# A changed start-up order in a tuned FFT-and-MLP kernel: table first, expanded matrices on two engines, weight clamp and second weight fold later

## Chip, cores and metric

One core of one Trainium2 chip. The metric is the device time of the core in microseconds (us); lower is better. The kernel before took 1937.98 us (median of 3 runs, 1937.06 to 1938.95). Ratios are the mean time of one kernel's fast runs over the mean of the other's fast runs of the same rounds, so they are not quite the ratio of the medians that are quoted; the interval in brackets is the 95% interval. Absolute times of different batches come from different chips, so every batch has its own runs of the kernel before.

## The reference

```python
x:     (8, 3008, 256)   float32
w_in:  (256, 2048),  w_out: (2048, 256)

X = np.fft.fft(x, axis=1)
X = np.fft.fft(X, axis=2)
y = X.real.astype(np.float32).reshape(8 * 3008, 256)

h = y @ w_in
g = h * (1.0 / (1.0 + np.exp(-1.702 * h)))
return (g @ w_out).astype(np.float32)          # (24064, 256)
```

The kernel does the long transform in two stages (3008 = 47 x 64), folds the short transform into `w_in` ahead of time ("weight folds"), and runs 384 hidden/activation/product steps. Nearly the whole run is those steps on TensorE. This study is about the first 80 us, in which the first transform stage, the rounding of the weights and the weight folds are done.

## The kernel before

These are the parts that the change and the argument touch. `pair` holds the expanded matrices of the first mixing, `room` the folded pieces of x.

```python
def matrices():                                     # 8 expanded matrices from the first table
    kinds = [w0[:, n0 + i:n0 + i + 1] for i in range(3)]
    tasks = iter((nc.scalar, nc.gpsimd, nc.vector) * 4)
    for s0, own, other in ((1, 0, 1), (17, 1, 0)):
        src = w0[:, s0 * NM:(s0 + 15) * NM].rearrange("p (s m) -> p s m", m=NM)
        for even in (1, 0):
            for c, kind in enumerate((own, other)):
                ...                                 # one scaled copy, 128 x 720, on next(tasks)

def fold_first(g):
    t, e = xt[0:2 * NA, 4 * g:4 * g + 4, :], room[g][0:2 * NA]
    nc.gpsimd.tensor_copy(free(e, 0, [D, 4], [H, 2]), free(t, 0, [D, 4], [H, 2]))   # corner copy, 94 x 8
    for at, op in ((1, ALU.add), (H + 1, ALU.subtract)):
        nc.vector.tensor_tensor(e[:, :, at:at + H - 1], t[:, :, 1:H],
                                free(t, D - 1, [D, 4], [-1, H - 1]), op=op)

def mix_first(i):                                   # 8 matmuls, then one copy by ScalarE
    ps, ns = bank("ps1"), (2 * i + 1, 2 * i + 2) if i < 7 else (0, 15)
    ...
    nc.scalar.copy(to, free(ps[:], 0, [D, 2], [1, D]))

def bounds(key, first=False):                       # "the clamp" of one weight chunk
    ...
    nc.gpsimd.tensor_scalar(m[:], hi, scalar1=TOP, scalar2=-TOP, op0=ALU.min, op1=ALU.max)   # m
    if first:
        nc.vector.tensor_tensor(g[:], hi, hi, op=ALU.mult)                                   # g
    else:
        nc.scalar.activation(g[:], hi, ACTF.Square)                                          # g
    nc.scalar.activation(r[:].bitcast(F32), lo, ACTF.Copy, scale=2.0 ** -29, bias=2.0 ** 23) # r
    nc.scalar.activation(r[:], r[:].bitcast(F32), ACTF.Copy, bias=-2.0 ** 23)                # r

# rounded(): m, a, a on VectorE; finish(): wst = a + r on GpSimd

def fold_w(n):                                      # psw: 4 matmuls; wcs copies; psf: 4; af copy
    for cs in range(2):
        ps = bank("psw")
        for i in range(2):
            nc.tensor.matmul(ps[:], lhsT=cd[:, i, cs, :], rhs=wst[n][:, i, :], start=(i == 0), stop=(i == 1))
        nc.scalar.copy(wcs[cs][...], ...)
    ps = bank("psf")
    for f in range(4 * n, 4 * n + 4):               # weights with a single row
        nc.tensor.matmul(ps[:, f:f + 1], lhsT=wcs[1][0:1, f * 128:f * 128 + 128], rhs=twos[:], ...)
    nc.scalar.copy(af2[:, 4 * n:4 * n + 4], ps[:, 4 * n:4 * n + 4])

def nyquist(b, blk):                                # for the first block only:
    row = pqt[b, blk][0:1, 1, :]
    ps = bank("psn")
    nc.tensor.matmul(ps[:], lhsT=ones[:], rhs=row, start=True, stop=True)    # ones is 1 x 128
    nc.scalar.copy(nb[:], ps[:])
```

The start-up order:

```python
nc.scalar.dma_start(out=w0, in_=tab1[:, 0:n0 + 4])            # first table, 802 KB
for part in ((0, 4), (28, 32), (4, 8), (24, 28), (8, 16), (16, 24)):
    load_first(*part)                                         # x, on SyncE's queue
...
warm(7)
matrices()
for i, need in enumerate(((0, 7), (1,), (6,), (2,), (5,), (3,), (4,), ())):
    for g in need:
        fold_first(g)
    mix_first(i)
    ...
    if i == 4:
        bounds(("in", 0), True)                               # clamp of chunk 0 inside the mixing
...                                                           # spills, refill
round_in(0)
finish_in(0)
bounds(("in", 1), True)
round_in(1)
finish_in(1)
fold_w(0)
warm(3)
bounds(("out", 0))
round_out(0)
finish_out(0)
rotate(0, 0, 4)                                               # the small copy t
stage2(0, 0)                                                  # transform of the first block: pq
fold_w(1)
bounds(("in", 2))
...
ahead = [("in", 2), ("out", 1), ("in", 3), ("out", 2), ("out", 3)]
for t, (kind, c) in enumerate(ahead):
    at(t, round_out if kind == "out" else round_in, c)
    if t + 1 < len(ahead):
        at(t, bounds, ahead[t + 1])
    at(t + 1, finish_out if kind == "out" else finish_in, c)
early[2], early[4] = 2, 3                                     # folds 2 and 3 inside the step loop
```

In the step loop, step t does: hidden(t) (pa, pb on TensorE, v on ScalarE); nyquist if t is 0; product; `fold_w(early[t])`; activate; rows(t) (h, dif, h on VectorE, which free the banks pa and pb); then what `at` put there.

Of the kernel before, what the change touches and what calls it, by code (L numbers as in the profile page):

```python
# [35 lines left out]
NJ = NB // 2  # L36
NM = 48
# [9 lines left out]
def view(ap, offset, *dims):  # L47
    return bass.AP(ap.tensor, ap.offset + offset, [list(d) for d in dims])


def free(ap, offset, *dims):
    return bass.AP(ap.tensor, ap.offset + offset, [list(ap.ap[0])] + [list(d) for d in dims])
# [8 lines left out]
def tables(S, D):  # L61

    assert S == NA * NB and D == 256
    H = D // 2
    ks = np.array([kp(u, a) for a in range(NG) for u in range(NU)])
    s = NB * np.arange(NA)[:, None, None] + np.arange(NB)[None, :, None]
    angle = 2.0 * np.pi * ((s * ks) % S) / S
    cos, sin = np.cos(angle), np.sin(angle)
    w1 = np.zeros((NA, NJ + 3, NG * NU, 2))
    w1[:, 1:NJ, :, 0], w1[:, 1:NJ, :, 1] = cos[:, 1:NJ], sin[:, 1:NJ]  # L70
    e0, o0, e1, o1 = ENDS
    w1[:, e0, :, 0], w1[:, o0, :, 0], w1[:, e1, :, 1], w1[:, o1, :, 1] = cos[:, 0], sin[:, 0], cos[:, NJ], sin[:, NJ]


    w0 = np.zeros((128, NJ + 1, NG * NU, 2))
    low, high = w0[0:2 * NA:2], w0[1:2 * NA:2]
    low[:] = w1[:, :NJ + 1]
    high[:, 1:NJ, :, 0], high[:, 1:NJ, :, 1] = cos[:, NJ + 1:], -sin[:, NJ + 1:]
    high[:, e0, :, 1], high[:, o0, :, 1] = cos[:, NJ], sin[:, NJ]
    odd = np.arange(128)[:, None] % 2  # L80
    kinds = np.concatenate([1.0 - odd, odd, -1.0 * odd, 1.0 - 2.0 * odd], 1)

    c, q = np.divmod(np.arange(NJ), 16)
    m2 = []
    for jj in np.where(q, np.where(c, NJ - q, q), 16 * c), 4 * (q // 2) + 2 * (q % 2) + c:
        j, k2 = jj[:, None], np.arange(NB)[None, :]
        beta = 2.0 * np.pi * ((j * k2) % NB) / NB
        m = np.zeros((NU, 2, NJ, 2, NB))
        m[:, 0, :, 0], m[:, 1, :, 0] = np.cos(beta), -np.sin(beta)
        m[:, 0, :, 1], m[:, 1, :, 1] = np.sin(beta), np.cos(beta)  # L90
        m[:, :, 0, 0] = m[:, :, 0, 1] = np.stack([np.ones(NB), 1.0 - 2.0 * (np.arange(NB) % 2)])
        m2.append(m)
    rot = np.zeros((NU, 2, NJ, NU, 2, NJ))
    for i in range(NU):
        for n in range(NJ):
            rot[i, 0, n, i, 1, n], rot[i, 1, n, i, 0, n] = (1.0, -1.0) if n else (0.0, 0.0)
        rot[i, 0, 0, i, 0, 0] = rot[i, 1, 0, i, 1, 0] = 1.0

    m, d = np.arange(D)[:, None], np.arange(H)[None, :]
    phi = 2.0 * np.pi * ((m * d) % D) / D  # L100
    cd = np.stack([np.cos(phi), -np.sin(phi)], 1)
    cd[:, 1, 0] = 1.0 - 2.0 * (np.arange(D) % 2)
    cd = cd.reshape(2, H, 2, H).transpose(1, 0, 2, 3)
    small = [t.reshape(128, -1) for t in (*m2, rot, cd)]
    pad = 64 - NM
    w1 = np.pad(w1.reshape(NA, -1), ((0, 128 - NA), (0, pad)))
    w0 = np.concatenate([w0.reshape(128, -1), np.zeros((128, pad)), kinds], 1)
    return np.concatenate([w0, w1], 1).astype(np.float32), np.concatenate(small, 1).astype(np.float32)
# [3 lines left out]
def kernel(ctx: ExitStack, tc, x, w_in, w_out, tab1, tab2, out):  # L112
    nc = tc.nc
    B, S, D = x.shape
# [19 lines left out]
    Td = [nc.dram_tensor(f"Td{b}", (NG * 128, D), F32, kind="Internal").ap() for b in range(B)]  # L134
# [18 lines left out]
    def bank(name):  # L153
        return psm.tile([128, 512], F32, tag="mm", name=name)
# [6 lines left out]
    xt = xp.tile([128, NJ, D], F32, tag="x", name="xt")  # L161
# [69 lines left out]
    def matrices():  # L231

        kinds = [w0[:, n0 + i:n0 + i + 1] for i in range(3)]
        tasks = iter((nc.scalar, nc.gpsimd, nc.vector) * 4)
        for s0, own, other in ((1, 0, 1), (17, 1, 0)):
            src = w0[:, s0 * NM:(s0 + 15) * NM].rearrange("p (s m) -> p s m", m=NM)
            for even in (1, 0):
                for c, kind in enumerate((own, other)):
                    out, by = pair[:, even, s0:s0 + 15, c * NM:(c + 1) * NM], kinds[kind if even or not kind else 2]
                    eng = next(tasks)  # L240
                    if eng is nc.scalar:
                        eng.activation(out, src, ACTF.Copy, scale=by)
                    else:
                        eng.tensor_scalar(out, src, scalar1=by, scalar2=None, op0=ALU.mult)  # L244
# [14 lines left out]

    def mix_first(i):  # L260

        ps, ns = bank("ps1"), (2 * i + 1, 2 * i + 2) if i < 7 else (0, 15)
        for at, n in enumerate(ns):
            for even in range(2):
                c0, c1 = (0, H + 1) if even else (H + 1, D)
                o = ps[:, at * D + c0:at * D + c1]
                for k, slot in enumerate((n, NJ - n if n else 16)):
                    rhs = room[slot // 4][:, slot % 4, c0:c1]
                    w = free(pair[:, even, slot], 0, [1, 128])
                    nc.tensor.matmul(o, lhsT=w, rhs=rhs, start=(k == 0), stop=(k == 1))  # L270
        to = free(xt[:], ns[0] * D, [(ns[1] - ns[0]) * D, 2], [1, D])
        nc.scalar.copy(to, free(ps[:], 0, [D, 2], [1, D]))

    def spill_first(lo, hi):
        for c, eng in enumerate((nc.sync, nc.scalar)):
            eng.dma_start(out=view(Td[0], (16 * c + lo) * D, [NJ * D, NM], [1, (hi - lo) * D]),
                          in_=xt[NM * c:NM * c + NM, lo:hi, :].rearrange("p q d -> p (q d)"))

    def load_matrices():
# [74 lines left out]
    def bounds(key, first=False):  # L354


        hi, lo = raw[key][:, :, 1].bitcast(F32), raw[key][:, :, 0]
        g = sp.tile([128, 1024], F32, tag="s", bufs=3, name="g")
        m = cv.tile([128, 1024], F32, tag="m", bufs=2, name="m")
        r = cv.tile([128, 1024], U32, tag="r", bufs=2, name="r")  # L360
        nc.gpsimd.tensor_scalar(m[:], hi, scalar1=TOP, scalar2=-TOP, op0=ALU.min, op1=ALU.max)  # L361

        if first:
            nc.vector.tensor_tensor(g[:], hi, hi, op=ALU.mult)
        else:
            nc.scalar.activation(g[:], hi, ACTF.Square)
        nc.scalar.activation(r[:].bitcast(F32), lo, ACTF.Copy, scale=2.0 ** -29, bias=2.0 ** 23)
        nc.scalar.activation(r[:], r[:].bitcast(F32), ACTF.Copy, bias=-2.0 ** 23)
        pre[key] = g, m, r
# [22 lines left out]
    def round_in(n):  # L392
        wst[n] = op.tile([128, 2, 512], F32, tag="os", name="wst")
        out = wst[n][:].rearrange("p i f -> p (i f)")
        last["in", n] = rounded(lambda *ins: [(out, ins)], ("in", n))
# [10 lines left out]
    def finish_in(n):  # L406
        last["in", n]()
# [177 lines left out]
    n0 = (NJ + 1) * NM + 64 - NM  # L585
    flat = wot[:].rearrange("p w a q n -> p (w a q n)")
    pair = flat[:, 0:2 * NJ * 2 * NM].rearrange("p (e s m) -> p e s m", e=2, s=NJ)
    w0 = flat[:, 6176:6176 + n0 + 4]
# [5 lines left out]
    nc.vector.memset(wcs[0][:, 0:512], 1.0)  # L594
    for i, e in enumerate(rooms):

        (nc.vector, nc.gpsimd)[i % 2].memset(e[64:128], 0.0)
    nc.vector.memset(flat[:, 6144:6176], 0.0)
    nc.vector.memset(free(pair[:, 0, 0], 0, [2 * NJ * NM, 2], [16 * 2 * NM, 2], [1, 2 * NM]), 0.0)
    nc.vector.memset(ones[:], 1.0)  # L600
    nc.vector.memset(twos[:], 2.0)
    nc.scalar.dma_start(out=w0, in_=tab1[:, 0:n0 + 4])
    for part in ((0, 4), (28, 32), (4, 8), (24, 28), (8, 16), (16, 24)):
        load_first(*part)
    load_in(0, nc.sync)
# [6 lines left out]
# [4 lines that stand above are left out]
        if i == 2:  # L616
            specials()
        if i == 3:
            spill_first(1, 9)
            load_out(0, nc.sync)  # L620
        if i == 4:
            bounds(("in", 0), True)
        if i == 5:
            spill_first(9, 13)
    spill_first(13, 16)
    spill_first(0, 1)
    fill(0, 0, 4)
    load_in(2, nc.sync)
    load_out(1, nc.sync)
    round_in(0)  # L630
    finish_in(0)
    bounds(("in", 1), True)
    round_in(1)
    finish_in(1)
    fold_w(0)
    warm(3)
    bounds(("out", 0))
# [1 line left out]
    finish_out(0)  # L639
    rotate(0, 0, 4)  # L640
    stage2(0, 0)
    fold_w(1)
    bounds(("in", 2))

    extra, early = {}, {}

    def at(t, fn, *args):
        extra.setdefault(t, []).append((fn, args))

    n = len(steps)  # L650

    ahead = [("in", 2), ("out", 1), ("in", 3), ("out", 2), ("out", 3)]
    for t, (kind, c) in enumerate(ahead):
        at(t, round_out if kind == "out" else round_in, c)
        if t + 1 < len(ahead):
            at(t, bounds, ahead[t + 1])
        at(t + 1, finish_out if kind == "out" else finish_in, c)
    early[2], early[4] = 2, 3
    at(1, fill, 0, 4, NG)
    for t, load, c in ((0, load_in, 3), (1, load_out, 2), (2, load_out, 3)):  # L660
        at(t, load, c, nc.sync)
# [76 lines left out]
```

## Time and profile before

| kernel before | value |
|---|---|
| median of 3 runs | 1937.98 us |
| span of the profiled execution | 1935.6 us |
| TensorE idle in it | 21.6 us |
| mixing ends / first r / first fold starts | 33.3 / 28.5 / 33.3 us |
| hidden group 0 / v of step 1 / third fold | 50.5 / 58.0 / 62.4 us |
| hidden group 3, from where TensorE hardly stops | 69.4 us |

How to read it: in the chain of waits each line is start, duration, engine, tile and line of the kernel; each piece was released by the one above it. The timeline's lines are start, busy time, engine, line, operation, tiles, shapes, and in brackets the idle time before it with what ended it. "DVE" is VectorE, "ACT" ScalarE, "POOL" GpSimd, "PE" TensorE; psw is a weight fold. Each matmul of the code stands as two records in these traces (`warm(7)` shows as x14), and counts such as x8 are of records. A granted clock of 1.00 is full, 0.50 is half. A bank is an output buffer of the matmuls; a spill writes mixed rows to DRAM, and the refill reads them back. The lines themselves are in the prediction below.

### The profile page before, as it was taken

What the parts mean: (1) busy time and instruction counts of PE and PEld (TensorE: products, weight loads), DVE (VectorE), ACT (ScalarE), POOL (GpSimd) and SP (SyncE); (2) the same over time, 40 slices, a digit from 0 to 9 for tenths busy, and PEclk for the clock granted to TensorE, in tenths of its full rate; (3) what the DMA queues carried; (4) which work ended last, traced back from release to release, by engine and by line L of the source; (5) the groups of instructions that cost most, each with busy time, mean ns of one, the idle gap of its engine ahead of it and who ended that gap; (6) DMA issues with size and microseconds to landing.
All of it is one profiled execution on the core that took longest, in us unless ns stands there. A gap on an engine that the chain in (4) does not pass through costs nothing.

```text
span 1935.6 us, 29331 instructions
## 1 busy us (share of the span) xinstructions
PE 1914.0 (99%) x10722; PEld 1680.3 (87%) x10722; DVE 1417.6 (73%) x2935; ACT 670.4 (35%) x920; POOL 771.3 (40%) x1064
## 2 busy tenths in 40 slices
PE   8899999999999999999999999999999999999998
PEld 5698888988889888898889888898888988889887
DVE  6667777777778777876777777777777777777776
ACT  3633333333333333333333333333333333333332
POOL 5455223642246322462225522255223643223222
PEclk8999999999999999999999999999999999999999
DMA  8720460227203362025422263221720223202201
GB/s 257 183 49 10 94 80 12 49 52 115 17 12 59 48 110 17 20 51 97 61 25 50 33 95 47 24 49 43 114 26 13 18 45 59 17 12 27 17 12 23
DMA packets 144689, 103.54 MB, mean 53 GB/s; under 512 B 104739, under 2 KB 127651, under 8 KB 143073
## 3 DMA queue, kind: packets, MB, share of 16 engines
q1 hardware_dynamic: 143056, 99.79, 31.1%
q10 hardware_dynamic: 1488, 1.87, 0.3%
q8 instruction: 85, 1.39, 0.3%
q14 instruction: 60, 0.48, 0.1%
HBM read 58.38 MB, written 48.01 MB: 55 GB/s over the span
## 4 chain that ended last, share of the span: by engine, by line
PE 97%; DVE 1%; POOL 1%; issue 0%; ACT 0%; DMA 0%; POOLq 0%
PE po L521 59%; PE pa L454 17%; PE pb L454 17%; PE ps L213 1%; PE ps L319 1%; PE psw L423 1%; PE ps L270 1%; DMA wo<-in_tab_dram 0%; PE ps L217 0%; POOL wst L385 0%; POOL wo L244 0%; DVE m L378 0%; PE psf L430 0%; DVE a L381 0%; POOL m L361 0%
## 5 line engine op out<-in xcount | busy, mean ns | idle before, releaser
L521 PE MATMUL po<-s,wo 128*128 128x256 f32 (+1 forms) x3008 | 759.0, 375 | 0.0
L495 POOL TENSOR_TENSOR s<-h 128x256 f32<-128x256 f32 (+1 forms) x376 | 270.3, 719 | 1100.8 <-ACT h L483 1036.1
L521 PE MATMUL po<-h,wo 128*128 128x256 f32 (+1 forms) x2384 | 689.9, 375 | 0.0
L521 PEld LDWEIGHTS po<-s,wo 128*128 128x128 f32 x3008 | 572.1, 190 | 63.9
L458 ACT COPY v<-pa 128x512 f32<-128x512 f32 (+1 forms) x384 | 221.7, 577 | 1066.9 <-PE pa L454 1066.9
L468 DVE TENSOR_TENSOR h<-v,pb 128x512 f32<-128x512 f32 (+1 forms) x384 | 258.9, 674 | 410.6 <-PE pb L454 399.5
L521 PEld LDWEIGHTS po<-h,wo 128*128 128x128 f32 x2384 | 453.5, 190 | 51.2
L483 ACT ACTIVATE h<-h 128x1024 f32<-128x1024 f32 (+1 forms) x384 | 400.8, 1044 | 18.6 <-DVE h L478 16.2
L454 PE MATMUL pa<-pq,wcs 128*128 128x256 f32 (+1 forms) x1536 | 394.1, 379 | 0.0
L454 PE MATMUL pb<-pq,wcs 128*128 128x256 f32 (+1 forms) x1536 | 387.8, 375 | 0.4 <-ACT nb L337 0.4
L471 DVE SCALAR_TENSOR_TENSOR dif<-nb,af,pb 128x256 f32<-128x256 f32 (+1 forms) x768 | 328.3, 469 | 0.0
L454 PEld LDWEIGHTS pa<-pq,wcs 128*128 128x128 f32 x1536 | 287.0, 190 | 46.6 <-issue 9.9
L454 PEld LDWEIGHTS pb<-pq,wcs 128*128 128x128 f32 x1536 | 292.1, 190 | 33.5 <-ACT nb L337 0.8
L496 POOL TENSOR_TENSOR s<-h 128x256 f32<-128x256 f32 (+1 forms) x376 | 276.1, 734 | 0.0
L478 DVE TENSOR_TENSOR h<-pa,dif 128x512 f32<-128x512 f32 (+1 forms) x448 | 265.5, 604 | 13.2
L499 DVE TENSOR_TENSOR s<-h,s 128x256 f32<-128x256 f32 (+1 forms) x376 | 199.0, 529 | 12.9
L498 DVE TENSOR_TENSOR s<-s,h 128x256 f32<-128x256 f32 (+1 forms) x376 | 179.6, 478 | 4.3 <-POOL s L495 4.3
L199 POOL TENSOR_TENSOR xt<-xt 111x510 f32<-111x510 f32 x56 | 73.6, 1314 | 4.4
L555 DVE TENSOR_TENSOR c<-u,po 128x256 f32<-128x256 f32 (+1 forms) x188 | 69.4, 410 | 1.6
L325 DVE STREAM_TRANSPOSE pq<-ps 128x256 f32<-128x256 f32 x96 | 34.6, 418 | 44.6 <-PE ps L319 44.6
L555 DVE TENSOR_TENSOR u<-u,po 128x256 f32<-128x256 f32 (+1 forms) x141 | 57.8, 410 | 9.5 <-ACT u L526 4.6
L538 DVE STREAM_TRANSPOSE os<-c 128x512 f32<-128x512 f32 x94 | 61.1, 687 | 0.1
(72 smaller groups left out, 518.4 us busy)
## 6 DMA issues: line engine op xcount, KB each, us to landing
out_dram<-os SPq DMA_DIRECT2D x284, 64.0 KB
Td<-xt SPq DMA_DIRECT2D x14, 768.0 KB
t<-Td SPq DMA_DIRECT2D x7, 1536.0 KB
xt<-in_x_dram SPq DMA_DIRECT2D x14, 512.0 KB
xt<-Xr SPq DMA_DIRECT2D x14, 512.0 KB
nb<-pq SPq DMA_DIRECT2D x23, 256.0 KB
out_dram<-os SPq DMA_DIRECT2D x96, 56.0 KB
Xr<-in_x_dram SPq DMA_DIRECT2D x7, 752.0 KB
```

The source lines that it names most:

```text
L454: nc.tensor.matmul(ps[:, i * 256:i * 256 + n], lhsT=wcs[cs][:, f * 128:(f + 1) * 128], rhs=pq[:, cs, ks], start=True, stop=True)
L458: nc.scalar.copy(two(v[:], n), two(pa[:], n))
L468: nc.vector.tensor_tensor(two(h[:], n), two(v[:], n), two(pb[:], n), op=ALU.add)
L471: nc.vector.scalar_tensor_tensor(dif[:, i * 256:i * 256 + n], nb[:, ks], af2[:, f:f + 1], pb[:, i * 256:i * 256 + n], op0=ALU.mult, op1=AL ...
L478: nc.vector.tensor_tensor(free(h[:], 512 + at + m - 1, [256, 2], [RUN, blocks], [-1, m]), *ins, op=ALU.add)
L483: nc.scalar.activation(g, g, ACTF.Gelu_apprx_sigmoid)
L495: eng.tensor_tensor(s1, a21, a22, op=ALU.add)
L496: eng.tensor_tensor(s3, a11, a21, op=ALU.subtract)
L498: eng.tensor_tensor(s2, s1, a11, op=ALU.subtract)
L499: eng.tensor_tensor(s4, a12, s2, op=ALU.subtract)
L521: nc.tensor.matmul(pot[q][:, i, :n], lhsT=lhs, rhs=rhs, start=(p == 0 and i == 0 and f == 0), stop=(p == NP - 1), skip_group_check=True)
L555: nc.vector.tensor_tensor(out_, i0, i1, op=how)
```

## The change

Its intent is to have the first transform start sooner and the first hidden step sooner. The first table gets SyncE's queue ahead of x. The eight expanded matrices are made by ScalarE and VectorE, not GpSimd. The rows of the mixing are renumbered so that a copy and a spill are single contiguous runs. The clamp of the first weight chunk leaves the mixing and goes behind its folds. The second weight fold goes behind hidden group 0.

```diff
@@ tables: row order for the first block
-    for jj in np.where(q, np.where(c, NJ - q, q), 16 * c), ...:
+    for jj in np.where(c, 16 + q, np.where(q, 16 - q, 0)), ...:
@@ matrices
-        tasks = iter((nc.scalar, nc.gpsimd, nc.vector) * 4)
+        tasks = iter((nc.scalar, nc.vector, nc.scalar, nc.scalar, nc.vector) * 2)
@@ mix_first, spill_first
-        ps, ns = bank("ps1"), (2 * i + 1, 2 * i + 2) if i < 7 else (0, 15)
+        ps, ns = bank("ps1"), (2 * i + 2, 2 * i + 1) if i < 7 else (0, 15)
-        nc.scalar.copy(to, free(ps[:], 0, [D, 2], [1, D]))
+        nc.scalar.copy(xt[:, 30 - 2 * i:32 - 2 * i, :].rearrange("p j d -> p (j d)"), ps[:])
...                                                  # spill offsets; which engine clears which room
-    nc.scalar.dma_start(out=w0, in_=tab1[:, 0:n0 + 4])
+    nc.sync.dma_start(out=w0, in_=tab1[:, 0:n0 + 4])
@@ mixing loop
-            spill_first(1, 9)
+            spill_first(24, 32)
-        if i == 4:
-            bounds(("in", 0), True)
         if i == 5:
-            spill_first(9, 13)
-    spill_first(13, 16)
-    spill_first(0, 1)
+            spill_first(20, 24)
+    spill_first(16, 20)
...
-    round_in(0)
-    finish_in(0)
-    bounds(("in", 1), True)
-    round_in(1)
-    finish_in(1)
+    for c in range(2):
+        bounds(("in", c), True)
+        round_in(c)
+        finish_in(c)
...
     stage2(0, 0)
-    fold_w(1)
-    bounds(("in", 2))
...
+    at(0, bounds, ahead[0])
-    early[2], early[4] = 2, 3
+    early[0], early[2], early[4] = 1, 2, 3
```

More of the change, by code (lines that the diff above doesn't have):

```diff
@@ L84, in tables @@
     m2 = []
-    for jj in np.where(q, np.where(c, NJ - q, q), 16 * c), 4 * (q // 2) + 2 * (q % 2) + c:
+    for jj in np.where(c, 16 + q, np.where(q, 16 - q, 0)), 4 * (q // 2) + 2 * (q % 2) + c:
         j, k2 = jj[:, None], np.arange(NB)[None, :]
@@ L270, in mix_first @@
                     nc.tensor.matmul(o, lhsT=w, rhs=rhs, start=(k == 0), stop=(k == 1))
-        to = free(xt[:], ns[0] * D, [(ns[1] - ns[0]) * D, 2], [1, D])
-        nc.scalar.copy(to, free(ps[:], 0, [D, 2], [1, D]))
+        nc.scalar.copy(xt[:, 30 - 2 * i:32 - 2 * i, :].rearrange("p j d -> p (j d)"), ps[:])
     def spill_first(lo, hi):
         for c, eng in enumerate((nc.sync, nc.scalar)):
-            eng.dma_start(out=view(Td[0], (16 * c + lo) * D, [NJ * D, NM], [1, (hi - lo) * D]),
+            eng.dma_start(out=view(Td[0], (16 * c + lo - 16) * D, [NJ * D, NM], [1, (hi - lo) * D]),
                           in_=xt[NM * c:NM * c + NM, lo:hi, :].rearrange("p q d -> p (q d)"))
@@ L595 @@
     for i, e in enumerate(rooms):
-        (nc.vector, nc.gpsimd)[i % 2].memset(e[64:128], 0.0)
+        (nc.vector if i % 3 == 0 else nc.gpsimd).memset(e[64:128], 0.0)
     nc.vector.memset(flat[:, 6144:6176], 0.0)
```

## The prediction

> **What bounds the kernel now.** I read the page first (busy shares, the slices, the chain that ended last), then the chain of waits piece by piece over the first 95 us, then the timeline and one-microsecond windows there.
>
> ```profile
> PE 1914.0 (99%) x10722; PEld 1680.3 (87%) x10722; DVE 1417.6 (73%) x2935; ACT 670.4 (35%) x920; POOL 771.3 (40%) x1064
> ...
> PE   8899999999999999999999999999999999999998
> ```
>
> TensorE is busy 1914.0 of 1935.6 us: 21.6 us idle in all. Only the first two slices (48.4 us each) are below 9 tenths. Busy time in windows of 5 us adds up to 55.4 of the first 70 us, so 14.6 us of the 21.6 lie there; from 70 us on TensorE hardly stops. The change touches only work before that point and leaves TensorE's work the same. So its worth is the shift of the moment when TensorE becomes saturated (the fourth group of hidden matmuls, 69.4 us), and can't exceed about 15 us, 0.8%. The chain of waits over the start:
>
> ```profile
> 12.67 3.00 POOL wo L244
> 15.68 0.04 issue
> 15.72 12.28 PE ps L270 x78
> 28.00 0.02 issue
> 28.02 0.58 ACT xt L272
> 28.61 1.11 ACT r L367
> ...
> 30.88 2.35 POOL wst L385
> ...
> 45.21 3.65 PE psw L423 x8
> 48.85 0.02 issue
> 48.88 0.59 ACT wcs L425
> ...
> 50.67 1.16 ACT g L366
> ...
> 59.94 2.38 POOL wst L385
> 62.31 0.04 issue
> 62.36 5.41 PE psw L423 x8
> ```
>
> The reader is to see three stretches: the expanded matrices (GpSimd, until 15.68); the first mixing (TensorE), handing over to ScalarE's first rounding op r and the first rounded weight chunk wst; then weight folds psw, each waiting for a chunk. The matrices in the timeline:
>
> ```profile
> 7.80 2.47 ACT L242 ACTIVATE wo<-wo 128x720 f32<-128x720 f32 x3 [1.09 <-DMA wo<-in_tab_dram]
> 7.80 1.83 DVE L244 TENSOR_SCALAR wo<-wo 128x720 f32<-128x720 f32 x2 [1.30 <-DMA wo<-in_tab_dram]
> 7.96 7.71 POOL L244 TENSOR_SCALAR wo<-wo 128x720 f32<-128x720 f32 x3 [3.62 <-DMA wo<-in_tab_dram]
> ```
>
> All three wait for the table until 7.8; ScalarE needs 0.82 us for one, VectorE 0.92, GpSimd 2.57.
>
> [...] after TensorE's idle time from 9.6 us the windows show a clock of 0.50 from 12 to 22 us, again from 39.3 to 42.7 and 63.2 to 66.6, each a multiple of 3.41 us. [...] those 2.57 us fell beside two-input folds, and the 128x1024 clamp m on GpSimd took from 1.10 to 2.16 us. [...]
>
> **The change, part by part.**
>
> Table first: the slices show 63 GB/s in the first 3 us, then about 343. 802 KB alone are moved by about 4.8 us; with some 1 us to land I take 6.0 instead of 7.78. The pieces of x after the first come no sooner: the bytes ahead of them are the same.
>
> Matrices: five on ScalarE, 6.0 + 5 x 0.82 = 10.1; three on VectorE, 6.0 + 3 x 0.92 = 8.8, then four folds of 0.71 (six took 4.25), to 11.6. So mixing starts at 11.6 instead of 15.72, 4.1 us sooner.
>
> Mixing: 128 records; 58 took 6.64 us at full clock, so 14.7 us. Before, 6.5 us of it ran at half clock. Now TensorE rests only about 2 us ahead of it, and I take the clock as full. The last piece of x landed at about 18.4, its folds end at 19.8, about 1 us after TensorE wants them. VectorE also no longer puts the clamp's 1.23 us ahead of the last folds. Mixing ends near 27 instead of 33.2, some 6 us sooner.
>
> Where that stops: before, ScalarE did r of chunk 0 between mixing copies (28.50). In the built order of the changed kernel it stands behind the last mixing copy and a spill: 27.1 + 0.6 + 0.4 = 28.1. Two ops (2.2) and wst (2.35) give 32.7 instead of 33.2. Only 0.5 of 6 us is left, and TensorE now idles from 27 to 32.7, enough to be put to half clock. The first psw, 3.7 us before, then takes 5.3 to 6, to about 38.5 (before 37.0). A wcs copy (0.6), psf (1.05), the bias copy, then ScalarE's g of the next chunk (1.1) and VectorE's m, a, a (1.24 + 0.71 + 1.24) lead to the small copy t: about 45, before 44.3.
>
> The single-run spills save one DMA issue on each of two queues, and the last spill comes some 6 us sooner; but at 43.07 TensorE did not wait for the refill, it was in its warm-up matmuls. Worth 0.
>
> The second fold (psw 3.65, its copies, psf 1.05) moves behind hidden group 0. That starts 1.8 us after t, near 47 instead of 50.5: 3.5 us gained. Given back at once: in the built order ScalarE now has v of step 0, nb, the three copies of the second fold, g, r, r of input chunk 2, g, r, r of output chunk 1, and only then v of step 1. Before, the first g, r, r stood ahead of v of step 0. From 47: hidden 1.9, psn 1.05, psw 3.45, copy 0.6, psf 1.05, bias copy 0.2, with about 1 us of hand-overs, reach 56; six ops of 1.09 reach 62.5, so v of step 1 comes at 62.5 to 63 instead of 57.98. The third fold's psw writes banks that step 1's VectorE ops (0.69 + 0.86 + 0.69) must free: in the built program it waits on VectorE. It starts near 64.7 instead of 62.36. TensorE rested before it as before, so I keep the 7.1 us from there to hidden group 3: 71.8 instead of 69.4.
>
> Walking all engines through the built order and its waits with these durations gives the same, 71.7 to 74.0 depending on where the clock windows fall, mean 72.9; the same walk of the kernel before gives 69.9 to 71.7, mean 70.8 (the trace: 69.4). The difference, +2.1 us, is less biased than either. After it TensorE has the same order and no idle time in which to recover: 1937.98 + 2 = **1940.0**.
>
> **Rivals.**
>
> The early gain gets through: if r of chunk 0 were not held by the last mixing copy, or the second fold's move counted alone, 3 to 6 us would be saved: 1932 to 1935. For it: the chain of waits runs through exactly the pieces shortened. Against it: ScalarE's in-order queue, and the chunk chain r, wst, m, a, a, wst, which has not become shorter.
>
> Nothing moves: the third fold starts when chunk 2 is ready, and that hardly moves (m of chunk 2 at 56.56 before; 56 to 57.6 by the sum above). If the banks did not wait for step 1, the time would be 1937 to 1938.
>
> The clock: if the mixing too falls into a half-clock window, its end, r, wst and all that follow come 1 to 4 us later: 1941 to 1944. For it: a rest of about 2 us against windows of 3.41 us whose place differs from run to run. The three runs before spread over 1.9 us, as my walk does by moving the windows alone.
>
> Transfers: r of chunks 2 and 1 frees raw buffers 3 to 5 us later (57 before), so output chunks 2 and 3, the second tables and the next x come later. x had its last issues at 75 us and is first folded after 110, the chunks have about 5 us to spare: I expect 0.
>
> **Range and chances.** The three runs spread by +-1 us; my walk missed the trace of before by 0.8 us. The sum rests most on the bank wait and on clock windows, some 2 us each way, with a longer tail towards faster, because a change like this is usually kept for a reason. So 1936.0 to 1942.5. 2% is 38.8 us, more than all idle time of TensorE: within 2% is all but certain.
>
> **What would show it.** Right: matrices without GpSimd done by about 10; first mixing matmuls at 11 to 12, their end near 27; first r at 28 or later; first psw near 32.7 at lower clock; hidden group 0 near 47; v of step 1 beyond 61; third psw at 64 or later behind a VectorE wait; hidden group 3 at 71 to 74; the rest of the span unchanged. Wrong: group 3 ahead of 69; mixing matmuls at 0.2 us a record; a table landing after 7; a refill that TensorE waits for; or a stall after 75 us for a late transfer.

## The result, and the profile after

The changed kernel took 1942.67 us (median of 6 runs, 1940.84 to 1947.98), the kernel before 1937.78 in the same rounds (6 runs, 1937.06 to 1939.37): ratio 1.0028 [1.0015, 1.0041]. Within 2% it is the same; it is also clearly a little slower. A second batch on another chip gave 1941.24 (5 runs) against 1938.72 (9 runs). So the cost is 2.5 to 4.9 us, where I had said 2.0. The first median lies 0.2 us above my range, the second inside it.

The runs of the changed kernel in the first batch spread over 7.1 us, those of before over 2.3. The profiled execution was the slowest of the six (1947.98), which has to be kept in mind: it shows the tail, and the second batch's profile (1941.98) is closer to the usual case.

The page of the changed kernel, busy shares and TensorE's slices:

```profile
PE 1920.2 (99%) x10722; PEld 1681.4 (86%) x10722; DVE 1415.1 (73%) x2935; ACT 672.5 (35%) x922; POOL 767.1 (39%) x1062
...
PE   7899999999999999999999999999999999999998
```

TensorE runs the same 10722 instructions but is busy 6.2 us longer (1914.0 before), and the span is 1946.2 us, 10.6 longer. The same instructions taking longer point to the clock; the other 4.4 us are idle time. Only the first slice has become emptier.

The chain of waits over the start of the changed kernel (start, duration, what):

```profile
8.69 4.49 POOL first L256
...
13.22 16.88 PE ps L270 x122
...
31.14 1.13 ACT r L366
...
33.44 2.37 POOL wst L384
...
35.85 5.74 PE psw L422 x8
...
49.56 1.50 PE pa L453 x4
51.06 1.71 PE pb L453 x4
52.77 2.00 PE psn L335 x2
54.77 6.47 PE psw L422 x8
...
69.47 0.48 ACT v L457
...
71.60 6.61 PE psw L422 x8
```

The reader is to see three things. The mixing is first held by a tiny GpSimd copy ("first", L256) of 4.49 us, which was no part of the chain before. The first r stands behind the end of the mixing, as predicted. From 49.56 to 61.2 hidden group 0, psn and the second fold run at about half speed: pa 1.50 and pb 1.71 for four records each (1.13 and 0.86 in the chain of e0, the repeat run below), psn 2.00, the fold 6.47. Summed over the 10 us from 50 to 60, TensorE is busy 10.00 us at a mean granted clock of 0.51.

The matrices in the timeline of the changed kernel:

```profile
5.63 4.04 ACT L242 ACTIVATE wo<-wo 128x720 f32<-128x720 f32 x5
5.63 2.70 DVE L244 TENSOR_SCALAR wo<-wo 128x720 f32<-128x720 f32 x3 [0.21 <-DMA wo<-in_tab_dram]
```

The table landed by 5.63 instead of 7.80, and the matrices were ready at 9.7 instead of 15.7, as intended.

The corner copies of `fold_first`, with count, then shortest/median/longest duration in ns, then the first and last start; first the changed kernel, then before:

```profile
L256 POOL COPY first<-xt x3: 192/197/4477, 7.3 to 13.1; 94x8 f32<-94x8 f32 x3
```

```profile
L256 POOL COPY first<-xt x3: 192/646/656, 15.6 to 16.8; 94x8 f32<-94x8 f32 x3
```

The same copy of 94x8 elements took 0.19 us or 4.48 us. It now runs beside eight back-to-back two-input folds on VectorE (8.25 to 13.11) and ended at 13.17, 0.06 us after the last of them; in e0 below it was 13.08 after 13.02, and in e11 a copy of 6.01 us ended at 15.95, after folds until 15.90. Before, GpSimd came to it later. That VectorE caused it fits, but no run isolated it.

From hidden group 3 on, nothing changed: span minus start of group 3 is 1866.2 us before and 1866.3 after (1866.4 in the second profile). No transfer stalls later. The whole difference is where group 3 starts: 69.4 before, 79.9 in the first profile after, 73.8 in the second.

### The profile page after: what moved, and what is told of

Same layout as the page of the kernel before. It is cut to its first block, busy times and chain, and to the rows that moved or that the text cites. A ratio compares the mean times of both kernels' runs of the same rounds, so it can differ in the third digit from the quotient of the medians.

```text
span 1946.2 us, 29330 instructions
## 1 busy us (share of the span) xinstructions
PE 1920.2 (99%) x10722; PEld 1681.4 (86%) x10722; DVE 1415.1 (73%) x2935; ACT 672.5 (35%) x922; POOL 767.1 (39%) x1062
## 3 DMA queue, kind: packets, MB, share of 16 engines
q10 hardware_dynamic: 1280, 1.05, 0.2%
## 4 chain that ended last, share of the span: by engine, by line
PE 98%; ACT 1%; DVE 0%; DMA 0%; POOL 0%; issue 0%; SPq 0%; ACTq 0%; DVEq 0%
PE po L520 59%; PE pa L453 17%; PE pb L453 17%; PE ps L213 1%; PE ps L318 1%; PE psw L422 1%; PE ps L270 1%; DMA xt<-in_x_dram 0%; PE ps L217 0%; POOL first L256 0%; PE psf L429 0%; ACT g L365 0%; DVE m L377 0%; ACT wcs L424 0%; POOL wst L384 0%
## 5 line engine op out<-in xcount | busy, mean ns | idle before, releaser
L498 DVE TENSOR_TENSOR s<-h,s 128x256 f32<-128x256 f32 (+1 forms) x376 | 200.4, 533 | 12.9
L554 DVE TENSOR_TENSOR c<-u,po 128x256 f32<-128x256 f32 (+1 forms) x188 | 69.4, 410 | 1.6
```

The lines of the kernel that those rows point to most:

```text
L498: eng.tensor_tensor(s4, a12, s2, op=ALU.subtract)
L554: nc.vector.tensor_tensor(out_, i0, i1, op=how)
```

## The experiments

**Theories.** (A) Order, the prediction's: r waits for the mixing's end, v of step 1 for a queue of ScalarE work, and the third fold for the banks of step 1; the parts cost what the sum said. (B) Clock: the new order leaves TensorE gaps, and half-clock windows that start in them set the time and its spread. (C) The corner copy on GpSimd, by its 4.5 us, holds the mixing. (D) A late transfer. D fell with the constant rest of the span above.

### e0 to e3: undoing the two moves

e0 is the changed kernel again. e1 undoes the move of the second fold, e2 that of the clamp, e3 both.

```diff
# e1 (e3 has both)
     stage2(0, 0)
+    fold_w(1)
+    bounds(("in", 2))
-    at(0, bounds, ahead[0])
-    early[0], early[2], early[4] = 1, 2, 3
+    early[2], early[4] = 2, 3
# e2
+        if i == 4:
+            bounds(("in", 0), True)
-    for c in range(2): bounds(("in", c), True); round_in(c); finish_in(c)
+    round_in(0); finish_in(0); bounds(("in", 1), True); round_in(1); finish_in(1)
```

> The changed kernel once more, so that its spread is known on this chip. Theory (order: the moved clamp and the moved second fold make the start longer, and where the clock windows fall adds 0 to 4 us): 1941 to 1946, mean near 1943, about 5 us above the kernel before; the group of hidden matmuls that saturates TensorE at 72 to 79 us, the GpSimd corner copy of room 7 again about 4 us long. Rival (the profiled execution was an accident of the clock and the change itself costs nothing): a mean within 1 us of the kernel before.

> Only the second weight fold and the bounds of input chunk 2 go back to before the first hidden group. Theory (six ScalarE ops now stand between the second fold and step 1's v, and the third fold's banks wait for step 1): about 2 us faster than the changed kernel, near 1941, v of step 1 about 61.5 instead of 65. Rival (the second fold's place costs nothing, since chunk 2 bounds the third fold anyway): the same as the changed kernel within 0.5 us.

> Only chunk 0's clamp goes back to beside the fifth mixing step. Theory (r of chunk 0 held behind the last mixing copy is the larger loss, because the chain r, wst, m, a, a, wst starts with it [...]): about 5 us faster than the changed kernel, near 1938, first r at about 24 instead of 31, first weight fold at about 30 instead of 36. Rival (only the clock in the mixing matters, which this does not mend): within 1 us of the changed kernel.

> Both orders go back; what stays of the change is the table ahead of x, the matrices without GpSimd and the single-run spills. Theory: the early parts are a true gain of 2 to 3 us over the kernel before that the two moves lose: 1935 to 1936.5. Rival (the early parts gain nothing or lose, because the GpSimd corner copy takes the place of the GpSimd matrices): 1938 or more.

| same chip, before 1938.72 | median us | ratio to before | first r | group 0 | group 3 (profile) |
|---|---|---|---|---|---|
| e0: both moves | 1941.24 | 1.0014 [1.0000, 1.0028] | 29.6 | 48.9 | 73.8 |
| e1: clamp moved only | 1939.81 | 1.0005 [0.9993, 1.0018] | 28.7 | 52.1 | 72.0 |
| e2: fold moved only | 1939.05 | 1.0001 [0.9989, 1.0014] | 22.3 | 45.2 | 69.9 |
| e3: neither | 1938.10 | 0.9996 [0.9984, 1.0009] | 22.6 | 50.1 | 70.1 |

Against e3 the clamp's move costs 1.7 us and the fold's 1.0 by the medians, in intervals that overlap, so neither cost is shown alone; neither pays. With the clamp inside the mixing the first r comes at 22.3 to 22.6, else at 28.7 or later: that step of the prediction holds. For e3 I had expected a gain of 2 to 3 us, and that was a miss: the early part alone is worth almost nothing (-0.6 us, inside the noise). With r at 22.6, its first fold still starts at 32.27, behind chunk 0's VectorE work and a wst of 3.20 us, not behind the mixing.

The chain of waits in e0 shows that its mixing still ended late, at 28.6, and that its first and third fold ran at half clock for most of their time:

```profile
13.13 15.43 PE ps L270 x122
...
34.31 6.65 PE psw L422 x8
...
48.94 1.13 PE pa L453 x4
...
65.97 6.17 PE psw L422 x8
```

The timeline of TensorE in e0, at the same place as the slow stretch above:

```profile
49.91 1.03 PE L453 MATMUL pb<-pq,wcs 128*128 128x256 f32 x4
50.86 1.12 PE L335 MATMUL psn<-pq,ones 1*128 1x512 f32 x2
51.91 3.70 PE L422 MATMUL psw<-wst,small 128*128 128x512 f32 x8
```

The same matmuls in the same order, at full clock: the fold took 3.70 us instead of 6.53. Nothing in the program differs, so this stretch is no fixed cost of the order; it is a state that some executions fall into. That speaks for B.

### e11 and e12: one half of the change on the kernel before

```diff
# e11, against before: only the engines of the matrices
-        tasks = iter((nc.scalar, nc.gpsimd, nc.vector) * 4)
+        tasks = iter((nc.scalar, nc.vector, nc.scalar, nc.scalar, nc.vector) * 2)
# e12, against before: only the two moves (clamp, second fold), none of the early parts
```

> The kernel before with only the matrices split between ScalarE and VectorE. Theory (GpSimd's matrices hold the mixing 4 us; freed, the early gain reaches the end in part as long as the clamp stays among the mixing copies): mixing starts for good at 13.4, first weight fold at 30.5 to 32, 1 to 2 us faster than the kernel before. Rival (the last piece of x and the chunk chain bound the first fold): within 0.5 us of it.

> The kernel before with only the two moves (all of chunk 0's clamp behind the mixing, second fold behind the first hidden group), without the table, the matrices and the spills. Theory (the moves lose and the early parts only soften it): with mixing ending at 33 or later, first r at 34 to 38 and first weight fold at 38 to 43; 8 to 12 us slower than the kernel before, 1946 to 1950. Rival (the moves are harmless, and the loss of the whole change comes from the early parts, such as the held corner copy): within 2 us of the kernel before.

e11: 1937.88 against 1937.99, ratio 1.0000 [0.9988, 1.0013]; the matrices alone show no gain (I had expected 1 to 2 us, which the interval of 2.5 us each way does not exclude). e12: 1945.71 (1944.36 to 1947.56) against 1937.18, ratio 1.0042 [1.0030, 1.0055], the largest effect of all. Its chain of waits shows why:

```profile
15.77 17.68 PE ps L270 x126
...
34.97 1.13 ACT r L367
...
37.26 2.37 POOL wst L385
```

With the matrices still late, the mixing ends at 33.4, and the moved clamp makes r wait for all of it. So by the medians the parts are not additive: the moves alone cost 8.5 us, the early parts alone give 0.6 (e3), together they cost 2.5 to 4.9. The times alone leave this at the edge of the noise; the chain above gives the reason, an early start that makes up for part of what the moves cost.

### e4: the corner copy (theory C)

```diff
-        nc.gpsimd.tensor_copy(free(e, 0, [D, 4], [H, 2]), free(t, 0, [D, 4], [H, 2]))
+        nc.vector.tensor_copy(free(e, 0, [D, 4], [H, 2]), free(t, 0, [D, 4], [H, 2]))
```

> The changed kernel with the corner copies (94x8) of the first folds on VectorE instead of GpSimd. Theory (one GpSimd copy [...] delays the first mixing matmuls to 12.5 to 13.2 and lets the clock fall during mixing; that was the first step missed by the prediction): mixing starts for good at about 11.5 and ends at 27, 1 to 2 us sooner than in the changed kernel, and the run is 1 to 2 us faster than it, about 1 us slower than the kernel before. Rival (the copy is hidden, since the last piece of x bounds the mixing's end): unchanged, 2.5 us or more above the kernel before.

1941.37 (1939.51 to 1945.41) against 1938.45, ratio 1.0017 [1.0004, 1.0029]: no better than the changed kernel. The mixing started at once and ended at 26.8, but in e5 and e6, which have the slow copy (1.80 us in e5, 4.49 in e6) and full clock there, it also ended at 26.9. The chain of e4 over the mixing runs through the last piece of x (landed at 18.0) and its folds (until 19.5). So the copy runs beside the wait for x, which lasts longer, unless the clock also falls at the pause it makes, as in the first profile, where the mixing ran at half clock from 12.6 to 19.5 and ended at 30.1. C falls as a cause of its own.

### e5, e6, e8, e13: filling TensorE's gaps (theory B)

`keep(n)` issues n extra matmuls into a bank that nobody reads; the outputs are unchanged. e5 fills ahead of the first fold, e8 only ahead of the first block's transform, e6 both of these and ahead of the third fold. e13 is e6 with the corner copy on VectorE.

```diff
+    def keep(n):
+        ps = pso.tile([128, 2, 256], F32, tag="o3", name="keep")[:].rearrange("p i f -> p (i f)")
+        for _ in range(n):
+            nc.tensor.matmul(ps, lhsT=small[:, 0:128], rhs=small[:, 0:512], start=True, stop=True)
+    keep(6)                  # e5, e6, e13: ahead of fold_w(0)
     fold_w(0)
     ...
     rotate(0, 0, 4)
+    keep(2)                  # e6, e8, e13
     stage2(0, 0)
     ...
+        if t == 2:
+            keep(6)          # e6, e13: ahead of the third fold
```

> The changed kernel with six matmuls of no use between the end of the mixing and the first weight fold, where TensorE idles 5.8 us. Theory (the idle time makes the clock fall, and the first fold then takes 5.4 to 6.6 us instead of 3.7, on the chain to the first hidden group): the first fold takes 3.7 us, the first hidden group comes 1.5 to 2.5 us sooner, and about 1 to 1.5 us are saved in the end. Rival (VectorE's and ScalarE's chunk chain sets that group, not the fold): first fold faster, but the hidden group and the time unchanged.

> The same, and two idle-filling matmuls before the first transform of the second stage and six before the third weight fold. Theory (TensorE's half-clock windows are the second part of the loss): all folds take 3.7 us, no half-clock window between 30 and 75 us, and 3 to 4 us are saved against the changed kernel: 0 to 1 us below the kernel before. Rival (order alone): at most 1 us saved.

> The changed kernel with only two idle-filling matmuls ahead of the first transform of the second stage, where TensorE waits for the copy t. Theory (with the second fold moved away, TensorE has nothing to do there, the clock may fall for some 10 us, and then the first hidden groups and the second fold run at half clock; that is the part of the slowdown that the prediction mis-sized): no half-clock window begins between 43 and 58 us, the second fold takes 3.7 us, no run above 1943, median near 1940. Rival (the fold's place in the order alone, at any clock): the second fold may still take 6.5 us, or the runs spread up to 1945 and more as in the changed kernel.

> The changed kernel with idle-filling matmuls at all three places and the corner copies on VectorE: against the run with the same filling and the copies on GpSimd (1938.67) it shows what the held copy costs at full clock. Theory now (the copy costs nothing then, since the last piece of x bounds the mixing's end; it only endangers the clock): 1937.5 to 1939, mixing ends at 26.8 in both. Rival (the copy was worth 1.5 us, as the first theory had it): 1936 to 1937.

| kernel | median us (range) | before | ratio | half clock in the first 85 us of its profile |
|---|---|---|---|---|
| e5 | 1944.02 (1940.59 to 1944.97) | 1938.45 | 1.0024 [1.0011, 1.0036] | 43.7 to 57.4, 67.6 to 74.4 |
| e8 | 1940.73 (1940.03 to 1942.14) | 1937.99 | 1.0015 [1.0002, 1.0027] | 30.6 to 37.4, 61.3 to 68.2 |
| e6 | 1938.67 (1937.22 to 1940.49) | 1938.45 | 0.9998 [0.9984, 1.0011] | 69.8 to 73.3 |
| e13 | 1937.93 (1936.96 to 1942.26) | 1937.18 | 1.0007 [0.9994, 1.0021] | none |

e5 was a miss of mine: the first fold did take 3.70 us, but the clock then fell at the next gap, where TensorE waits 2.35 us for the copy t, and the slow stretch of group 0 came back (psw 6.50). Filling this one gap only moved the fall to the next. With all three filled (e6, e13) no loss to before is left that could be told from noise: by the ratios e6 is 0.4 us faster and e13 1.4 us slower, with intervals from 3.1 us faster to 4.1 us slower. e5 and e6 ran side by side, and the slowest run of e6 (1940.49) is below the fastest of e5 (1940.59). e8, with only the gap ahead of group 0 filled, has no slow stretch there and no run above 1942.14. e13 against e6 is also the test of the corner copy at full clock: the mixing ended at 26.9 in both, and the ratios do not differ beyond their intervals.

TensorE's timeline in e13, whose profile has no half clock at all up to 1931 us:

```profile
32.72 3.70 PE L428 MATMUL psw<-wst,small 128*128 128x512 f32 x8 [0.67 <-POOL wst L390]
...
62.67 3.67 PE L428 MATMUL psw<-wst,small 128*128 128x512 f32 x8
...
69.07 1.13 PE L459 MATMUL pa<-pq,wcs 128*128 128x256 f32 x4
```

This is the changed order (with the corner copy on VectorE) with the clock taken out: group 3 at 69.07, against 69.41 in the kernel before (which has its own half-clock windows). So the order by itself neither wins nor loses against what before showed (e9 below, which is before with its third fold at full clock, has 68.5, some 0.6 us sooner), and what the changed kernel loses beyond it is clock: 4.7 us in e0's profile, 10.8 in the first.

### e7: v of step 1 ahead of the next chunk's rounding (theory A)

```diff
 for t, (kind, c) in enumerate(ahead):
+        if t == 1:
+            at(1, bounds, ahead[1])
-        if t + 1 < len(ahead):
+        if 0 < t and t + 1 < len(ahead):
```

> The changed kernel with the bounds of output chunk 1 moved behind v of step 1 on ScalarE. Theory (the third fold waits for banks that step 1's VectorE work frees, so v of step 1 is on the path): v of step 1 comes about 3.3 us sooner, the third fold 1 to 2 us sooner, at about 64 instead of 66, bounded then by chunk 2's wst; in the end 0 to 1.5 us faster, as output chunk 1 and input chunk 3 come later. Rival (wst of chunk 2 alone releases the third fold): v sooner, the third fold no sooner.

1940.92 (1939.75 to 1947.61), ratio 1.0017 [1.0004, 1.0031]. In the profile v of step 1 came at 62.7 instead of 69.4, and group 3 at 74.8 in spite of the slow stretch (46.7 to 57.0). But 1871.0 us followed it instead of 1866.2, so nearly 5 us were given back: later windows at 74.0 to 80.9 and 94.5 to 97.9 ran at half clock. The run does not separate A from B.

### e9, e10, e14: looking for a version better than both

```diff
# e9, against before
+        if t == 2:
+            keep(5)              # ahead of the third fold
# e10, against the changed kernel: corner copy on VectorE (e4); second fold back (e1);
#      only the two r operations of chunk 0 inside the mixing; and
+    keep(1)                      # ahead of fold_w(0)
+        if t == 2:
+            keep(5)
# e14: e10 and
+    keep(3)                      # ahead of stage2(0, 0)
```

> The kernel before with five idle-filling matmuls ahead of the third weight fold, where it idles 4.4 us. Theory (half-clock windows at folds cost in either kernel): the third fold takes 3.7 instead of 5.4 us and the run is 1.5 to 2 us faster, near 1936.7. Rival (wst and VectorE bound the time from there on): unchanged.

> The changed kernel with the second fold back, r of chunk 0 alone (ScalarE) back among the mixing copies while its other clamp work stays behind the folds, corner copies on VectorE, and idle-filling matmuls ahead of the first (one) and third (five) fold. Theory: mixing ends at 27, first weight fold at 29.5 to 30, third fold at 60 at full clock, saturation at 65 to 66 instead of 69.4: 4 to 5 us below the kernel before, 1933.5 to 1935. Rival (the early gain can't reach the third fold, since the chunk chain on VectorE and GpSimd is bound otherwise): within 1.5 us of the kernel before.

> The mixed version of the last job with three idle-filling matmuls ahead of the first transform of the second stage too, where its second fold took 5.4 us at half clock. Theory: second fold 3.7 us, first hidden group at 48 instead of 50, saturation about 1.5 us sooner than in the last job: 1934 to 1935, about 3.5 us below the kernel before. Rival (chunk 2 on ScalarE, VectorE and GpSimd bounds the third fold whatever the second does): 1936.

| kernel | median us (range) | before | ratio | group 3 |
|---|---|---|---|---|
| e9 | 1935.46 (1934.92 to 1938.50) | 1937.99 | 0.9989 [0.9976, 1.0003] | 68.5 |
| e10 | 1936.14 (1935.09 to 1938.15) | 1937.99 | 0.9992 [0.9980, 1.0005] | 67.2 |
| e14 | 1935.85 (1934.78 to 1937.71) | 1937.18 | 0.9993 [0.9981, 1.0006] | 67.5 |

All three lie 1.3 to 2.5 us below before by their medians, and none clearly: each interval includes 1. For e10 and e14 I had expected 1933.5 to 1935 and 1934 to 1935: misses. In their profiles a window within 83.7 to 88.7 us ran at half clock and about 2 us were given back (1867.9 to 1868.6 us after group 3).

### A count over all profiles

By then I had half-clock stretches in the first 95 us of nearly every profile, all multiples of 3.41 us. In the kernel before they ran from 12.00 to 22.24, 39.31 to 42.72 and 63.20 to 66.61, and these six times lie whole multiples of 3.413 us apart. The place of this grid differs: a first stretch began at 12.64 in the first profile after and at 12.93 in e0, the same kernel. So I laid a grid of 3.41 us through each profile that had one, from about 9 to 95 us, and counted for each window TensorE's busy time and the clock of the next window. Counting every matmul, no limit divides the windows: some fell after 2.7 us of work, and nine stayed at half clock though TensorE was shown busy for all of the window. All nine hold part of psn (eight windows) or psf (one), the two matmuls whose weights have a single row. Leaving those two out of the busy time (but counting the psn of 128 rows in e15 to e17 below), the windows divide, but for a band in which both happened:

| window (3.41 us) | next window | windows | counted busy time, us |
|---|---|---|---|
| full clock | falls to half | 50 | 0 to 1.76 |
| full clock | stays full | all others | 1.48 and more |
| half clock | stays half | 37 | 0 to 3.19 |
| half clock | rises to full | 52 | 2.97 and more |

So below 1.48 us of 3.41 the clock fell, and above 1.76 it did not; in between it fell after 11 windows and stayed after 44. It came back only after a window filled nearly to the end: 2.97 us or more, and with 2.97 to 3.19 us it came back after three windows and stayed down after two. That is a regularity of these traces, with ends of matmuls that are modelled. The choice to leave psf out rests on this count alone; psf also has a single column of data, so its row need not be the reason. For psn the part about single rows was tested:

### e15 to e17: psn with 128 rows

```diff
-    ones = const.tile([1, 128], F32, tag="ones", name="ones")
+    ones = const.tile([128, 128], F32, tag="ones", name="ones")
-    nc.vector.memset(ones[:], 1.0)
+    nc.vector.memset(ones[:], 0.0)
+    nc.vector.memset(ones[0:1, :], 1.0)
         row = pqt[b, blk][0:1, 1, :]
+        full = pqt[b, blk][:, 1, :]
-        nc.tensor.matmul(ps[:], lhsT=ones[:], rhs=row, start=True, stop=True)
+        nc.tensor.matmul(ps[:], lhsT=ones[:], rhs=full, start=True, stop=True)
```

The result and the shape of the output are the same; only the number of rows of the weights differs. e15 is the changed kernel with it, e16 is e4 with it, e17 is e5 with it.

> The changed kernel, with psn of the first block multiplied by 128 rows of weights (one row of ones, 127 rows of zeros; the same result) instead of a single row. Theory: [...] in the half-clock stretch of hidden group 0 neither of the two windows that psn touches lifts the clock. Then, where the clock falls ahead of or in group 0, the half clock lasts one window (3.4 us) if the fall comes with group 0, two at most; psn is then 1.1 to 2.1 us, the second fold's psw 3.7 to 4.5 instead of 6.5, hidden group 3 at 76 to 77 instead of 79.9, and the median of the timed runs lies 0.5 to 1.5 us under the 1941.2 to 1942.7 of before. Rival: rows do not matter; a stretch that begins there lasts 10.2 us again with psw at 6.5, and the median is 1941 to 1943. If the clock does not fall there in the profiled execution, this run says nothing of it.

> The same edit on the kernel with the corner copies on VectorE, whose half clock there ran from 47.2 to 57.4 us. Theory: from 47.2 to 50.6 only, psw 3.7 to 4 instead of 6.66, hidden group 3 at 73 to 74 instead of 76.7. Rival: 47 to 57 again, group 3 at 76 to 77.

> The same edit on the kernel with six fill matmuls ahead of the first fold, whose half clock there ran from 43.7 to 57.4 us (four windows; TensorE was busy 2.25 of 3.41 us in the first of them). Theory: from 43.7 to 50.5 (two windows), psw 3.7 to 4 instead of 6.5, hidden group 3 at 73 to 74 instead of 76.8, median 1 to 2 us under 1944. Rival: 43.7 to 57.4 again, group 3 at 76 to 77, median 1943 to 1945.

e16 is the clean test, since its clock fell at the same place as e4's. Windows of e4 and then of e16: the stretch in us, busy time (and instructions) of TensorE, its weight loads, VectorE, ScalarE and GpSimd, then the granted clock, the share of the DMA engines and GB/s.

```profile
44.00:47.20 3.20, 1.48 (x36) 1.14 (x37) 2.19 (x6) 0.00 (x0) 2.35 (x2) 0.99 0.90 341
47.20:50.60 3.40, 3.40 (x8) 1.78 (x6) 0.69 (x1) 0.58 (x1) 2.26 (x3) 0.50 0.83 278
50.60:54.00 3.40, 3.40 (x5) 1.17 (x4) 1.56 (x3) 0.58 (x1) 0.00 (x0) 0.50 0.02 6
```

```profile
44.00:47.40 3.40, 1.48 (x36) 1.14 (x37) 2.38 (x6) 0.00 (x0) 2.36 (x2) 1.00 0.92 336
47.40:50.90 3.50, 3.50 (x8) 2.19 (x7) 0.69 (x1) 0.58 (x1) 2.26 (x3) 0.51 0.77 262
50.90:54.30 3.40, 3.40 (x9) 1.33 (x7) 1.56 (x3) 1.17 (x2) 0.00 (x0) 1.00 0.02 7
```

The first lines are alike (1.48 us of work), the second too (TensorE busy all the time at half clock, the same eight matmul records). In e4 the clock stays at 0.50 for two more windows; in e16 it is back at 1.00 in the next. The second fold took 3.60 us instead of 6.66, and group 3 came at 71.8 instead of 76.7 (1.5 us of that is a faster third fold). It is one window of one execution; but no half-clock window that held a single-row psn came back in the next (eight of eight). e17 fell there too, for one window (45.7 to 49.1) in place of e5's four; its window ended as psn began, so it fits but does not test the rows. e15 did not fall there and says nothing of it (group 3 at 71.9).

On the time it showed little, against 1937.26 of before: e15 1940.00 (1939.88 to 1940.62), ratio 1.0013 [0.9998, 1.0028]; e16 1941.18, ratio 1.0019 [1.0005, 1.0032]; e17 1942.55, ratio 1.0025 [1.0012, 1.0039]. These ratios are those of e0, e4 and e5 within their intervals, and e17 still had a run of 1944.59. The slowest runs of e15 and e16 (1940.62 and 1942.04) are below those of the unedited kernels (1947.98 and 1945.41), which fits, with few runs.

## Why the prediction was right or wrong

- **Two misreadings.** "Only the first two slices" below 9 tenths overlooks the last, which is 8 too; it changes nothing. And "after TensorE's idle time from 9.6 us", said of the first fall in the kernel before, was read too kindly: none of the three windows ahead of its falls was idle. TensorE was busy in them for 1.43, 2.25 (of it 1.27 without psf) and 0.84 us. That a rest of 2 us is harmless was my assumption; no trace had shown it, and it was not.
- **Direction and bound: right.** A small loss, from a late start of group 3 and nothing after it.
- **Matrices and table: right.** Done at 9.7 (said 10.1); the table landed by 5.63 (said 6.0). In the trace its last packet ended at 4.92 (said 4.8), 0.7 us ahead; in the kernel before at 6.79, 1.0 us ahead of the landing at 7.78.
- **End of the mixing: right at full clock only.** "Mixing ends near 27": 26.5 to 27.6 in e1, e4 to e8 and e13, but 30.1 in the first profile and 28.6 in e0. I wrote "Now TensorE rests only about 2 us ahead of it, and I take the clock as full". There it was not, from 12.6 to 19.5 and from 12.9 to 16.3; the rival on the clock named this case.
- **r held by the mixing: right.** First r at 28.0 in e13 (said 28.1), first fold at 32.72 (said 32.7), and 22.3 to 22.6 for r where the clamp was put back. In the first profile TensorE idled 5.76 us ahead of the first fold, and the clock was 0.50 from 33.12 to 39.95: the fold took 5.74 us (said 5.3 to 6), with the gap filled (e5) 3.70.
- **The step that failed: the clock, taken as full in the mixing ("I take the clock as full") and in the stretch from group 0 to the second fold.** For the stretch the sum says "From 47: hidden 1.9, psn 1.05, psw 3.45", 6.4 us at full clock. In the first profile the same work took 11.7 (1.50 + 1.71 + 2.00 + 6.47). That is 5.3 us more, and with the 2.6 us by which group 0 itself was late, less an unused allowance for hand-overs, it makes up the 6.4 to 6.9 us by which v of step 1 (69.4, said 62.5 to 63) and the third fold (71.6, said 64.7) were late. The third fold at half clock adds 1.2. So group 3 came at 79.9, said 71.8. That is the slowest execution. In e0's profile (1941.98, nearer to the first median of 1942.67) the stretch ran at full clock, and what was mis-sized is the mixing, with the two folds that ran at half clock: the mixing's end at 28.6 (said 27), the first fold from 34.31 for 6.65 us (said 32.7, and 5.3 to 6), group 0 at 48.9 (said 47), the third fold 6.17 (said 5.4), group 3 at 73.8 (said 71.8). The terms of the order held in both: v of step 1 came 14.8 us after group 0 in e0 and 14.9 in e13 with the clock full, where the sum has 15.5 to 16.
- **Why it was mis-sized.** I moved the second fold out from between the transform and group 0 and counted only where it went. In its place TensorE waits 0.9 us for pq, and 1.2 us for t just ahead of that (0.2 before, where warm-up matmuls at half clock lasted until then). The window there then holds 0.8 to 1.5 us of work when the grid lies badly (after, e4, e5, e7, e12, e16, e17: seven of the ten profiles with the fold moved and nothing filled in), and the clock falls as group 0 begins or up to 2.3 us ahead of it (e5). The fold in its old place did not keep the clock from falling: in three of the six profiles that have it there with nothing filled in ahead of the transform (e9, e10, e11) it fell too. But there the half clock lasted one window, which the fold's matmuls filled or nearly filled (3.14 us of 3.41 in e11). With the fold moved it lasted three or four windows where the single row of psn fell into it (after, e4, e5, e7). That the row is the reason rests on the pair e4 and e16; that the fold's old place is what kept these falls short is read from these profiles and was not tested.
- **The range: wrong on its long side.** I put the longer tail towards faster, "because a change like this is usually kept for a reason", which is no reading of a profile. The rival on the clock, 1941 to 1944, is where the kernel is; it deserved the larger part, and its cost beyond the mixing was not in it.
- **Rivals.** "The early gain gets through" fell: no version with all of r behind the mixing came below before. "Nothing moves" fell. Transfers cost 0, as said.

Still open: how often an execution of the changed kernel meets each slow window, since only profiled executions show it; why the profiled execution was the slowest of its kernel in after, e0, e4, e5, e6, e7, e12 and e16; how much of the 2.5 to 4.9 us in the timed runs is the stretch at group 0 rather than the other windows; whether the 1.3 to 2.5 us of e9, e10 and e14 are real; and which of the mis-sized terms the execution of the median, 1942.67, had, since it was not profiled. Those fills together with psn of 128 rows were not run.

## What to carry to other kernels

When work is moved off a spot, look at what it leaves behind: here a fold of 3.7 us behind a gap went with half clock for one window, and short work with a single-row matmul in its place with half clock for up to four. Look for a grid of half-clock windows in the profile (here of 3.41 us), and ask at every gap how much work is left in a window at its worst place. Here the clock fell after every window with less than 1.48 us of counted work and after none with more than 1.76, and one to four windows at half speed followed: count them in the range if not in the middle. Test what you assume of the clock on the trace: in the windows ahead of the three falls of the kernel before, TensorE was busy for 1.43, 2.25 (1.27 counted) and 0.84 us. And shorten only what the next engine waits for: here an early mixing was worth 0.6 us alone, inside the noise, because the rounding of the first chunk had its own chain.
